# Threshold attention and an exact-GELU MLP on one core: diagonals moved to GpSimd, regrouping in longer runs, sums moved ahead

## The chip, the cores and the metric

The kernel runs on one core of a Trainium2 chip. The metric is the device time in microseconds (us) of one launch. Before the change it is 1428.99 us, the median of three runs (1428.49 to 1430.3). The profile was taken in another run, whose span is 1430.0 us.

Engines in the profile: PE is TensorE (matmuls), PEld its weight loads, DVE is VectorE, ACT is ScalarE, POOL is GpSimd, SP is SyncE, which here only issues DMAs. L12 is line 12 of the kernel.

## The reference

Attention with a threshold over 8 batches of 8 heads, 576 tokens, 64 channels; then an MLP with exact GELU on 4608 tokens, 512 to 2048 to 512 channels:

```python
scores = scale * np.matmul(q, k.transpose(0, 1, 3, 2))
thresh = np.max(scores, axis=-1, keepdims=True) - tau
scores = np.where(scores >= thresh, scores, -1000000000.0)
scores = scores - np.max(scores, axis=-1, keepdims=True)
attn = np.exp(scores)
attn = attn / (np.sum(attn, axis=-1, keepdims=True) + 1e-09)
o = np.matmul(attn, v)
x = o.transpose(0, 2, 1, 3).reshape(B * S, H * D)
h = x @ w_in
out = (0.5 * h * (1.0 + erf(h / sqrt(2)))) @ w_out
```

q, k, v are fp32. w_in and w_out lie in memory as 64-bit floats, so the kernel itself makes fp32 of them.

## The kernel before

**Order of work.** Heads are handled in pairs (A and B, the two halves of the 128 partitions): 32 pairs, four per batch. A pair has five slots: four chunks of 128 query rows and a tail of 64. In each slot TensorE makes the scores, VectorE the negated maximum, ScalarE Exp, VectorE the comparison with the threshold, the product and the sum of each row. Slots 0 to 19 are the first batch (pairs 0 to 3, called "early"); in them the weights are converted too, 32 pieces of 512 columns, part of them in each slot:

```python
def conversions():          # one piece; the yields are nanoseconds of VectorE
    vec.tensor_scalar(expo, hi, 0x7FF00000, None, op0=ALU.bitwise_and)           # L176
    nc.scalar.activation(power, expo, AF.Relu, bias=rebias, scale=8.0)           # L177
    yield 340
    vec.tensor_scalar(mant, top, 0x0FFFFFFF, 0x10000000, ...)                    # L183, the piece before
    yield 340
    vec.scalar_tensor_tensor(power, hi, 0x80000000, power, ...)                  # L185
    yield 720
    vec.scalar_tensor_tensor(dst, mant, 2.0 ** -28, power, ...)                  # L187
    load_piece()            # the next piece: two DMAs of 512 KB that GpSimd issues
    yield 700
```

Half of the pieces land in the first 2048 columns of the tiles `pd`, which from slot 20 on hold the turned p.

**Early pairs** divide p by its sum while they turn it: a matmul against a diagonal of the inverses. The slot's end, and what the next slot does with it:

```python
def softmax_tail(p, i):     # p = (scores >= threshold) * Exp, with the row sums in den
    nc.vector.scalar_tensor_tensor(row, sc, thr, row, is_ge, mult, accum_out=den[e])   # L386
    nc.gpsimd.tensor_scalar(den, den, 1e-9, None, op0=ALU.add)                         # L389

def diagonal(p, i):
    nc.vector.reciprocal(den, den)                                                     # L397
    for e in range(n):
        nc.scalar.activation(diag[:, e, :], ident, AF.Copy, scale=den[:, e:e + 1])     # L400

def turn_p_early(p, i):     # TensorE, in the next slot, behind its scores (L355)
    nc.tensor.matmul(tr, lhsT=w[:, cols], rhs=diag[:, e, :])                           # L301
    nc.scalar.copy(pT, tr)                                                             # L309
...
convert(3000 if n < 2 * HP else 3650 if n < BATCH - 1 else 1e9)     # end of each slot
if early:
    diagonal(p, i)
```

**Later pairs** turn p on VectorE in blocks of 32x32, and SyncE's DMAs bring the blocks to the partitions where the weighing of v needs them:

```python
def turn_p(p, i):           # pd[e] is [128, 20 blocks, 128]
    for e in reversed(range(n)):
        to = pd_tail[p % 2] if i == NC else pd[e][:, :, i * Q:(i + 1) * Q]
        nc.vector.transpose(to[:, 0:NB, :], w[:, e * S:(e + 1) * S] as [p, b, i])      # L433

def regroup(p, i):          # at i = 2 for chunks 0 and 1, at i = 3 for chunks 2 and 3, at 4 the tail
    half = slice((i - 1) * Q, (i + 1) * Q)
    for a in range(4):
        for e in (1, 0):
            nc.sync.dma_start(pT[e][:, :, a * P:(a + 1) * P][:, :, half], pd[e][rows, :, half])   # L448

def weigh_v(p, lo, hi):     # columns 0 to 288, 288 to 576
    nc.tensor.matmul(xT[f, 0:hi - lo], lhsT=v[:, e, c, :], rhs=pT[e][:, c, lo:hi])     # L460
    # then x = xT * inverse sums, on VectorE (L478)
```

**MLP.** Ten blocks of 256 tokens run as plain matmuls, cut into small steps that fill TensorE between the attention's (layer 1, L520; Gelu, L500, with the table of Exp loaded again behind it, L507; layer 2, L532). The last eight blocks, two by two, run with seven quarter products instead of eight (L641). For that, sums and differences of quarters are made on VectorE: of w_in in `weights_in()`, right behind the last slot, and four more of w_in and four of x at the start of the stage:

```python
fill(1e12, B * S)           # the rest of the plain blocks
strassen(*ext):
    vec.tensor_tensor(a, w_in_sb[c][:, low], a, op=ALU.subtract)     # 4 of them, L612
    x_sums(*DUOS[0])                                                 # 4 of them, L653 to L656
    for each duo of blocks: ...                                      # products, L641
    # out in rows of 512 channels, one DMA of 256 KB per 128 tokens (L744, L749)
```

Of the kernel before, what the change touches and what calls it, by code (L numbers as in the profile page):

```python
# [18 lines left out]
def kernel(  # L19
# [69 lines left out]

    ident = const.tile([P, P], FP32, name="ident")  # L90
# [5 lines left out]
    pd = [const.tile([P, 4 * KR, P], FP32, name=f"pd{e}") for e in range(2)]  # L96
# [6 lines left out]
    for t in pd:  # L103
        nc.gpsimd.memset(t[:, NB:4 * KR, :], 0.0)
# [32 lines left out]
    def load_piece():  # L137
        if loaded[0] == len(pieces):
            return
        dst, src = pieces[loaded[0]]  # L140
        loaded[0] += 1
        if not wide:
            nc.sync.dma_start(dst, src)
            converted[0] += 1
            load_piece()
            return
        k = loaded[0] - 1
        if k % 2:

            room = pd[k // 2 % 2][:, 0:NB - 2, :].bitcast(U32).rearrange("p b i -> p (b i)")  # L150
            raw, shifted = room[:, 0:2 * PIECE], room[:, 2 * PIECE:4 * PIECE]
        else:
            raw, shifted = (xg.tile([P, 2 * PIECE], U32, tag="x", name=s) for s in ("raw", "shifted"))
        nc.gpsimd.dma_start(raw, src.bitcast(U32))
        n = 8 * PIECE - 4
        nc.gpsimd.dma_start(shifted.bitcast(U8)[:, 0:n], src.bitcast(U8)[:, 3:3 + n])
        raws.append((dst, raw, shifted))
# [78 lines left out]
    def load_early(p):  # L236
        b, hp = divmod(p, HP)
        s = st[p] = {}
        for name, src in (("q", q), ("k", k)):
            t = s[name] = ld.tile([P, NC + 1, P], FP32, tag=name, name=name)  # L240
            eng = nc.scalar if p < 2 and name == "k" else nc.sync
            for e in range(2):
                eng.dma_start(
                    t[:, 0:NC, e * D:(e + 1) * D],
                    src[b, 2 * hp + e, 0:MAIN, :].rearrange("(t p) d -> p t d", p=P),
                )
            eng.dma_start(
                t[0:TAIL, NC, :].rearrange("p (e d) -> p e d", e=2),
                src[b, 2 * hp:2 * hp + 2, MAIN:S, :].rearrange("e s d -> s e d"),
            )  # L250

    def load_v_early(p):
        b, hp = divmod(p, HP)
        t = st[p]["v"] = v_sb[p % 4]
        for e in range(2):
            nc.sync.dma_start(t[:, e, 0:NC, :], v[b, 2 * hp + e, 0:MAIN, :].rearrange("(t p) d -> p t d", p=P))
            nc.sync.dma_start(t[e * TAIL:(e + 1) * TAIL, e, NC, :], v[b, 2 * hp + e, MAIN:S, :])
# [134 lines left out]
    def diagonal(p, i):  # L392

        s = st[p]
        den = s.pop(("sum", i))
        n = den.shape[1]
        nc.vector.reciprocal(den, den)  # L397
        diag = s["diag", i] = dg.tile([P, 2, P], FP32, tag="inv", name="diag")
        for e in range(n):
            nc.scalar.activation(diag[:, e, :], ident, AF.Copy, bias=0.0, scale=den[:, e:e + 1])  # L400
# [22 lines left out]
    def turn_p(p, i):  # L423

        s = st[p]
        w = s.pop(("p", i))
        n = 1 if i == NC else 2  # L430
        for e in reversed(range(n)):
            to = pd_tail[p % 2] if i == NC else pd[e][:, :, i * Q:(i + 1) * Q]
            nc.vector.transpose(to[:, 0:NB, :], w[:, e * S:(e + 1) * S].rearrange("p (b i) -> p b i", i=Q))  # L433

    def regroup(p, i):

# [3 lines left out]
        for a in range(4):  # L440
            rows = slice(a * Q, (a + 1) * Q)
            if i == NC:
                e, at = divmod(a * Q, TAIL)
                nc.sync.dma_start(s["pT"][e][:, :, MAIN + at:MAIN + at + Q], pd_tail[p % 2][rows])
                continue
            half = slice((i - 1) * Q, (i + 1) * Q)
            for e in (1, 0):
                nc.sync.dma_start(s["pT"][e][:, :, a * P:(a + 1) * P][:, :, half], pd[e][rows, :, half])  # L448

    def weigh_v(p, lo, hi):  # L450
# [5 lines left out]
        for c in range(KR):  # L456
            for e in range(2):
                f = slice(e * D, (e + 1) * D)
                pT = s["pT"][0 if p < EARLY and c == NC else e]
                nc.tensor.matmul(  # L460
                    xT[f, 0:hi - lo], lhsT=s["v"][:, e, c, :], rhs=pT[:, c, lo:hi],
                    start=(c == 0), stop=(c == KR - 1))
# [29 lines left out]
    warm = const.tile([P, 2], FP32, name="warm")  # L492
    nc.vector.memset(warm, 0.0)

# [15 lines left out]
    def block_steps(n):  # L510

        g = {}
        for j in range(N_DF):
# [11 lines left out]
        for m in range(TOK // P):  # L525
            for j in range(N_DF):
                yield NS_OUT, len(pieces) - N_DF + j + 1
# [11 lines left out]
    mlp = {"n": 0, "steps": None, "next": None, "debt": 0.0}  # L539
# [41 lines left out]
    def weights_in():  # L581
# [3 lines left out]
        rest = [units(v_sb[i % 4])[0] for i in range(NP - 4, NP - 1)]  # L585
# [9 lines left out]
        return (s1, s2, s4), room + rest  # L595
# [11 lines left out]
    def strassen(ext, room):  # L607
        s1, s2, s4 = ext
        for h in range(HF // U):
            for c in range(NK):  # L610
                a = w_in_sb[c][:, HF + h * U:HF + (h + 1) * U]
                vec.tensor_tensor(a, w_in_sb[c][:, h * U:(h + 1) * U], a, op=ALU.subtract)  # L612
        room = room + units(v_sb[(NP - 1) % 4]) + [u for t in pd_tail for u in units(t)]
        room += [x for _ in range(2) for x in unit(xg, "x", 2)]
        x_ext = [room.pop().rearrange("p (c t) -> p c t", c=NK) for _ in range(3)]
        o_ext = [room.pop() for _ in range(2)]
        room += [x for _ in range(N_DF // 2 + 2) for x in unit(gp, "g")]
        room += [u for t in pd for u in units(t)]
# [30 lines left out]
        def x_sums(n1, n2):  # L649
            t1, t2, t4 = x_ext  # L650
            a, b = x_blk[n1], x_blk[n2]
            b11, b21, b12, b22 = a[:, 0:NK, :], a[:, NK:2 * NK, :], b[:, 0:NK, :], b[:, NK:2 * NK, :]
            vec.tensor_tensor(t1, b12, b11, op=ALU.subtract)  # L653
            vec.tensor_tensor(t2, b22, t1, op=ALU.subtract)
            vec.tensor_tensor(b12, b22, b12, op=ALU.subtract)  # L655
            vec.tensor_tensor(t4, b21, t2, op=ALU.subtract)  # L656

# [7 lines left out]

        def finish_chunk(j, x, p3):
# [6 lines left out]
        x_sums(*DUOS[0])  # L673
        for sb, (n1, n2) in enumerate(DUOS):
# [45 lines left out]
            for m in ms:  # L720
# [3 lines left out]
                vec.tensor_tensor(lo[m][:, 0:HD], lo[m][:, 0:HD], vs[m], op=ALU.add)  # L724
            for n in DUOS[sb + 1] if sb + 1 < len(DUOS) else ():
                if n in away:
                    bring(n)
            if sb + 1 < len(DUOS):
                x_sums(*DUOS[sb + 1])
# [7 lines left out]
            for m in ms:  # L737
                product(ys[m], rows(g22, m, wt4))
                vec.tensor_tensor(hi[m][:, 0:HD], hi[m][:, 0:HD], ys[m], op=ALU.add)
            for m in ms:  # L740
                product(xs[m], rows(gs1, m, wt1))
                vec.tensor_tensor(hi[m][:, HD:2 * HD], hi[m][:, HD:2 * HD], xs[m], op=ALU.add)
                row = n2 * TOK + m * P
                nc.sync.dma_start(out[row:row + P, :], hi[m])  # L744
            for m in ms:
                product(xs[m], rows(g12, m, w_out_part(1, 1)))
                nc.scalar.copy(lo[m][:, HD:2 * HD], xs[m])
                row = n1 * TOK + m * P
                nc.sync.dma_start(out[row:row + P, :], lo[m])  # L749

    load_early(0)
    load_early(1)
# [12 lines left out]
    BATCH = HP * SLOTS  # L765
    WEIGH = 2
# [18 lines left out]
    for n in range(len(slots) + WEIGH + 1):  # L785
# [15 lines left out]
        if p > EARLY and i == WEIGH:  # L801
            made = [weigh_v(p - 1, h * HALF, (h + 1) * HALF) for h in range(2)]
# [34 lines left out]
        if n == BATCH:  # L837
            for t in pd_tail:
# [7 lines left out]
        convert(3000 if n < 2 * HP else 3650 if n < BATCH - 1 else 1e9)  # L846
        if early:
            diagonal(p, i)
        if not early:
# [51 lines left out]
```

## Time and profile before

Busy shares and instruction counts are in the first part of the page; the 40 slices show them along the time, in tenths. The costliest groups that the change touches, from the page and the groups of lines:

| line | engine, what | count | mean ns |
|---|---|---|---|
| L400 | ScalarE, diagonal 128x128 | 36 | 392 |
| L389 | GpSimd, sum + 1e-9, 1 or 2 columns | 20 | 233 to 891 |
| L397 | VectorE, reciprocal of 1 or 2 columns | 20 | 150 to 170 |
| L176, L183 | VectorE, 128x512, one input | 64 | 417 to 443 |
| L185, L187 | VectorE, 128x512, two inputs | 64 | 683 to 692 |
| L433 | VectorE, 128x576 turned in blocks | 252 | 756 to 779 |
| L460 | TensorE, weighing v, 288 columns | 1120 | 128 |
| L448 | SyncE, regroup DMA of 160 KB | 448 | 3.9 us to landing |

(A fp32 matmul is two instructions. The 128 ns of L460 are its busy time, 143.2 us, by its count; those of the two heads overlap.) The chain that ended last is 85% TensorE, 6% VectorE, 5% ScalarE and 2% DMA. Read the waits as: which engine stood still, in front of which line, until which engine's line ended. A stretch is read as its length, then the busy time of each engine in it.

### The profile page before, as it was taken

Reading aid. Unit: us, or ns where it says so; the run is one execution under the profiler, and the core shown is the slowest. Engines: PE = TensorE matmul, PEld = TensorE weight load, DVE = VectorE, ACT = ScalarE, POOL = GpSimd, SP = SyncE. Lnnn points to the kernel's source line nnn. Section 1 sums busy time; section 2 is a strip of 40 time slices with the busy share of each in tenths; the row PEclk is TensorE's granted clock in tenths of the full one; section 3 lists DMA queues with packets and bytes.
Section 4 is the critical chain, followed back from the end, with each engine's and each line's share of the span. In section 5 each row is a group of like instructions: output and inputs, shape, how many; then the busy total and the mean of one; then the engine's idle time right before and its main releaser. Section 6 shows DMA issues by size and latency. Waiting matters only on the chain.

```text
span 1430.0 us, 19776 instructions
## 1 busy us (share of the span) xinstructions
PE 1385.1 (97%) x6544; PEld 960.9 (67%) x6544; DVE 900.0 (63%) x1908; ACT 640.8 (45%) x1039; POOL 389.1 (27%) x810
## 2 busy tenths in 40 slices
PE   5898999999999999999999999999999999999999
PEld 4666547566466574665746657466488888888887
DVE  5887787777767777777777777777654142241230
ACT  5758525436256373562745627457142141230320
POOL 4443244433434434434434344330000000000000
PEclk8999999999999999999999999999999999999999
DMA  9977167776667776677776777765500100100000
GB/s 260 297 264 241 40 144 150 152 150 133 131 137 145 153 147 133 142 140 159 156 140 143 160 154 152 142 135 100 107 0 1 44 1 0 59 1 8 22 1 30
DMA packets 449492, 167.06 MB, mean 117 GB/s; under 512 B 413040, under 2 KB 432048, under 8 KB 449392
## 3 DMA queue, kind: packets, MB, share of 16 engines
q1 hardware_dynamic: 423184, 108.65, 38.8%
q0 software_dynamic: 23808, 56.57, 12.9%
q8 instruction: 53, 0.87, 0.2%
q10 hardware_dynamic: 2400, 0.59, 0.2%
q14 instruction: 47, 0.39, 0.1%
HBM read 71.68 MB, written 11.47 MB: 58 GB/s over the span
## 4 chain that ended last, share of the span: by engine, by line
PE 85%; DVE 6%; ACT 5%; DMA 2%; issue 1%; SPq 1%; POOL 0%; DVEq 0%; ACTq 0%; POOLq 0%
PE bank L641 27%; PE hT L520 18%; PE o_ps L532 17%; PE sc L355 12%; PE xT L460 9%; ACT p L370 2%; DVE p L386 1%; PE tr L301 1%; DVE nmx L367 1%; DVE power L185 1%; ACT L500 1%; ACT diag L400 1%; DMA pd<-in_moe_w_in_dram 1%; ACT L507 0%; DVE expo L176 0%
## 5 line engine op out<-in xcount | busy, mean ns | idle before, releaser
L370 ACT ACTIVATE p<-sc,nmx 128x576 f32<-128x576 f32 x288 | 202.5, 739 | 384.4 <-DVE nmx L367 384.4
L367 DVE TENSOR_REDUCE nmx<-sc 128x1 f32<-128x576 f32 x288 | 205.0, 749 | 149.8 <-PE sc L355 149.8
L520 PE MATMUL hT<-x,w_in 128*128 128x256 f32 x1280 | 296.2, 384 | 0.0
L532 PE MATMUL o_ps<-w_out,g 128*128 128x512 f32 x640 | 295.1, 604 | 0.0
L520 PEld LDWEIGHTS hT<-x,w_in 128*128 128x128 f32 x1280 | 238.4, 190 | 56.9 <-issue 25.2
L386 DVE SCALAR_TENSOR_TENSOR p<-sc,thr,p 128x576 f32<-128x576 f32 x288 | 225.4, 816 | 65.2 <-ACT p L370 64.2
L368 POOL TENSOR_SCALAR thr<-nmx,tau_eff 128x1 f32<-128x1 f32 x288 | 85.0, 295 | 547.4 <-DVE nmx L367 544.9
L532 PEld LDWEIGHTS o_ps<-w_out,g 128*128 128x128 f32 x640 | 117.1, 190 | 141.0 <-issue 139.2
L355 PE MATMUL sc<-kT,qT 64*128 64x288 f32 x960 | 165.0, 432 | 2.6 <-DVE p L386 2.4
L460 PE MATMUL xT<-pT,v 128*64 128x288 f32 (+2 forms) x1280 | 164.4, 409 | 3.2 <-ACT g L500 3.2
L433 DVE STREAM_TRANSPOSE pd<-p 128x576 f32<-128x576 f32 x224 | 160.8, 756 | 2.9
L355 PEld LDWEIGHTS sc<-kT,qT 64*128 64x128 f32 x960 | 92.9, 187 | 84.2 <-issue 71.8
L460 PEld LDWEIGHTS xT<-pT,v 128*64 128x64 f32 x1280 | 90.2, 137 | 73.4 <-issue 13.5
L232 POOL DMA_DIRECT2D v<-in_v_dram x208 | 111.0, 537 | 10.5 <-issue 9.5
L641 PE MATMUL bank<-x,w_in 128*128 128x256 f32 x384 | 94.7, 383 | 3.2 <-DVE x L655 3.2
L507 ACT ACT_TABLE_LOAD x71 | 91.1, 1283 | 1.3
L500 ACT ACT_TABLE_LOAD x71 | 91.1, 1283 | 1.3
L641 PE MATMUL bank<-unit 128*128 128x256 f32 x352 | 88.6, 382 | 0.0
L641 PEld LDWEIGHTS bank<-x,w_in 128*128 128x128 f32 x384 | 73.7, 192 | 14.2 <-issue 4.1
L223 POOL DMA_DIRECT2D q<-in_q_dram x104 | 70.9, 686 | 15.9 <-issue 15.0
L641 PEld LDWEIGHTS bank<-unit 128*128 128x128 f32 x352 | 67.4, 192 | 9.4
L301 PE MATMUL tr<-diag,p 128*128 128x128 f32 (+1 forms) x360 | 51.8, 312 | 22.1 <-ACT diag L400 13.8
(143 smaller groups left out, 1346.4 us busy)
## 6 DMA issues: line engine op xcount, KB each, us to landing
pT<-pd SPq DMA_DIRECT2D x448, 160.0 KB, 3.9
pT<-pd_tail SPq DMA_DIRECT2D x112, 80.0 KB, 2.8
q<-in_q_dram POOLq DMA_DIRECT2D x104, 72.0 KB, 4.0
k<-in_k_dram POOLq DMA_DIRECT2D x104, 72.0 KB, 2.6
out_dram<-o_sb SPq DMA_DIRECT2D x28, 256.0 KB, 3.9
inv<-turned SPq DMA_DIRECT2D x56, 128.0 KB, 3.9
v<-in_v_dram POOLq DMA_DIRECT2D x156, 40.0 KB, 3.0
raw<-in_moe_w_in_dram POOLq DMA_DIRECT2D x8, 512.0 KB, 5.5
```

The lines of the kernel that those rows point to most:

```text
L232: eng.dma_start(t[r:P:4, e, 0:n, :], rows[:, r * KR:r * KR + n, :])
L355: nc.tensor.matmul(sc[e][:, h, 0:HALF], lhsT=lhsT, rhs=s["kT"][rows, at:at + HALF], start=True, stop=True)
L367: nc.vector.tensor_reduce(nmx[:, e:e + 1], sc, axis=AXIS.XY, op=ALU.max, negate=True)
L370: nc.scalar.activation(w[:, e * S:(e + 1) * S].rearrange("p (h s) -> p h s", h=2), sc, AF.Exp, bias=nmx[:, e:e + 1], scale=1.0)
L386: nc.vector.scalar_tensor_tensor(row, sc[e][:, :, 0:HALF], thr[:, e:e + 1], row, op0=ALU.is_ge, op1=ALU.mult, accum_out=den[e])
L433: nc.vector.transpose(to[:, 0:NB, :], w[:, e * S:(e + 1) * S].rearrange("p (b i) -> p b i", i=Q))
L460: nc.tensor.matmul(xT[f, 0:hi - lo], lhsT=s["v"][:, e, c, :], rhs=pT[:, c, lo:hi], start=(c == 0), stop=(c == KR - 1))
L500: nc.scalar.activation(t, hT, AF.Gelu)
L507: nc.scalar.activation(warm[:, 1:2], warm[:, 0:1], AF.Exp)
L520: nc.tensor.matmul(hT[:, j % 2, :], lhsT=w_in_sb[c][:, j * P:(j + 1) * P], rhs=x_blk[n][:, c, :], start=(c == 0), stop=(c == N_DM - 1))
L532: nc.tensor.matmul(o[:, 0:d_model], lhsT=g[j][:, m * P:(m + 1) * P], rhs=w_out_sb[j], start=(j == 0), stop=(j == N_DF - 1))
L641: nc.tensor.matmul(to, lhsT=l, rhs=r, start=start and k == 0, stop=k == len(pairs) - 1, skip_group_check=not start)
```

## The change

1. **Diagonals.** In the first batch GpSimd multiplies the identity by the inverse sums, no longer ScalarE, and the reciprocal and the diagonals come after the first 700 ns of the slot's conversion instead of after all of it. This is to have them earlier and to free ScalarE.
2. **Regrouping.** The turned p of both heads is one tile, laid out so that a head's half (two chunks) is 20 x 64 floats in a row; pT is laid out in groups of 64 query rows, [9 groups, 5, 64]. A regroup DMA then moves runs of 5 x 64 floats, 1280 bytes, instead of 256. Both heads are turned in one instruction. The weighing takes 320 and 256 columns, and its right operand is now pieces of 64 columns, 320 apart.
3. **Sums.** The last w_in differences and the first sums of x are made behind the last slot too, while the last plain block is in its layer 2, which no longer reads w_in.
4. **Smaller parts.** k and v of the early pairs are loaded by four rows per partition, so v comes in runs of 1 KB; the table of Exp is loaded at the start; the outputs of the last stage are stored by halves of 256 channels, each as soon as it is there; unused blocks of the turned tile are set to zero at slot 20, not at the start.

```diff
-    pd = [const.tile([P, 4 * KR, P], FP32, name=f"pd{e}") for e in range(2)]
+    turned_p = const.tile([P, 2, 2, 4 * KR, 2 * Q], FP32, name="turned_p")
+    pd = [turned_p[:, e, :, :, :].rearrange("p h b i -> p (h b i)") for e in range(2)]
...
+                order = "(t p) d -> p t d" if name == "q" else "(p t) d -> p t d"
...
-            nc.scalar.activation(diag[:, e, :], ident, AF.Copy, bias=0.0, scale=den[:, e:e + 1])
+            nc.gpsimd.tensor_scalar(diag[:, e, :], ident, den[:, e:e + 1], None, op0=ALU.mult)
...
-        for e in reversed(range(n)):
-            to = pd_tail[p % 2] if i == NC else pd[e][:, :, i * Q:(i + 1) * Q]
-            nc.vector.transpose(to[:, 0:NB, :], w[:, e * S:(e + 1) * S].rearrange("p (b i) -> p b i", i=Q))
+        if i == NC:
+            nc.vector.transpose(pd_tail[p % 2][:, 0:NB, :], w[:, 0:S].rearrange("p (b i) -> p b i", i=Q))
+            return
+        nc.vector.transpose(
+            turned_p[:, :, i // 2, 0:NB, i % 2 * Q:(i % 2 + 1) * Q], w.rearrange("p (e b i) -> p e b i", e=2, i=Q))
...
-                nc.sync.dma_start(s["pT"][e][:, :, a * P:(a + 1) * P][:, :, half], pd[e][rows, :, half])
+                nc.sync.dma_start(by_64(s["pT"][e])[:, 2 * a + h, :, :], turned_p[rows, e, h, :, :])
...
-                    xT[f, 0:hi - lo], lhsT=s["v"][:, e, c, :], rhs=pT[:, c, lo:hi],
+                    rhs = by_64(s["pT"][e])[:, lo // (2 * Q):hi // (2 * Q), c, :]
...
+        # (in weights_in, behind the last slot)
+        assert mlp["n"] == PLAIN and mlp["layer"] == 2
         for h in range(HF // U):
             for c in range(NK):
                 a = w_in_sb[c][:, HF + h * U:HF + (h + 1) * U]
                 vec.tensor_tensor(a, w_in_sb[c][:, h * U:(h + 1) * U], a, op=ALU.subtract)
+        x_sums(x_ext, *DUOS[0])
...
-                row = n2 * TOK + m * P
-                nc.sync.dma_start(out[row:row + P, :], hi[m])
+                store(n2, m, hi[m], HD)
...
     load_early(0)
+    nc.scalar.activation(warm[:, 1:2], warm[:, 0:1], AF.Exp)
...
-            made = [weigh_v(p - 1, h * HALF, (h + 1) * HALF) for h in range(2)]
+            made = [weigh_v(p - 1, lo, hi) for lo, hi in ((0, WIDE), (WIDE, S))]
...
-        convert(3000 if n < 2 * HP else 3650 if n < BATCH - 1 else 1e9)
+        share = 3000 if n < 2 * HP else 3650 if n < BATCH - 1 else 1e9
         if early:
+            convert(700)
             diagonal(p, i)
+            share -= 700
+        convert(share)
```

## The prediction

> **What bounds the kernel now.** I read four views in this order: engine totals and the 40 slices of the page, then busy time by stretch, then the waits and the chain of waits of the stretches where TensorE is not full, and last the timeline at the one gap late in the run.
>
> ```profile
> PE 1385.1 (97%) x6544; PEld 960.9 (67%) x6544; DVE 900.0 (63%) x1908; ACT 640.8 (45%) x1039; POOL 389.1 (27%) x810
> ...
> PE   5898999999999999999999999999999999999999
> ...
> DVE  5887787777767777777777777777654142241230
> ...
> DMA  9977167776667776677776777765500100100000
> ```
>
> TensorE (PE) has work for 1385.1 of 1430.0 us. So 44.9 us is all that can be won without taking work from it, and the change takes none. The stretches say where those 44.9 us are (columns: stretch, its length, busy us of each engine with instruction counts, granted clock, DMA share, GB/s):
>
> ```profile
> 20.00:40.00 20.00, 16.50 (x114) 12.71 (x114) 16.55 (x37) 14.86 (x32) 8.81 (x19) 0.84 1.03 306
> 40.00:60.00 20.00, 15.58 (x105) 12.37 (x106) 17.34 (x39) 14.52 (x31) 7.92 (x16) 0.84 1.07 287
> 97.00:165.63 68.63, 60.37 (x331) 44.88 (x329) 49.57 (x111) 53.06 (x90) 20.18 (x42) 0.93 0.57 182
> 600.00:700.00 100.00, 99.75 (x480) 60.90 (x480) 75.03 (x155) 53.11 (x71) 40.35 (x82) 1.00 0.70 144
> 1020.00:1040.00 20.00, 16.77 (x68) 9.88 (x67) 9.55 (x18) 2.96 (x5) 0.00 (x0) 0.84 0.24 58
> ```
>
> From about 200 us to 1020 us TensorE is full (99.75 of 100 us in the row shown), whatever DMA (share 0.70) and VectorE (75) do. The losses lie in the first 200 us (about 35 us of idle TensorE, 11.8 of them in the first 20 us, before data is there), at 1020 to 1040 us (3.2 us, clock 0.84), and after the last product (3.4 us).
>
> The first 20 slots, the first batch, run from 11.43 to 165.63 us. Their waits, first for 21 to 97 us, then for 97 to 166 us (engine and line that waited, what for, us in total, times, longest):
>
> ```profile
> PEld tr L301 <- ACT diag L400: 16.8, 8, 6.2
> PE tr L301 <- ACT diag L400: 13.2, 6, 5.6
> DVE p L386 <- ACT p L370: 4.9, 10, 1.1
> DVE expo L176 <- DMA raw<-in_moe_w_in_dram: 2.1, 1, 2.1
> ```
> ```profile
> PE tr L301 <- ACT g L500: 5.0, 4, 2.3
> DVE mant L183 <- ACT power L177: 6.2, 3, 3.6
> DVE nmx L367 <- PE sc L355: 4.9, 2, 3.7
> DVE p L386 <- ACT p L370: 3.9, 8, 0.9
> ```
>
> And three steps of the chain of waits (start, us, what):
>
> ```profile
> 34.50 0.46 DVE expo L176
> 35.06 0.55 issue
> 35.61 0.68 ACT diag L400 x2
> 36.32 0.75 ACT p L370
> ```
>
> The reader is to see that TensorE waits for the diagonals, the diagonals stand in ScalarE's queue, and behind them in the same queue stands the Exp of the next slot, for which VectorE then waits. Until 97 us VectorE is nearly the bound (67.3 of 75.4 us busy, summed over slots). After that ScalarE joins it: Gelu with two table loads (1.28 us each) comes into every slot.
>
> Last, the join of the plain blocks and the seven-product stage, in the timeline:
>
> ```profile
> 1030.31 1.03 PE L641 MATMUL bank<-x,w_in 128*128 128x256 f32 x4
> 1034.34 0.69 DVE L656 TENSOR_TENSOR unit<-x,unit 128x512 f32<-128x512 f32 x1
> 1034.57 2.04 PE L641 MATMUL bank<-x,w_in 128*128 128x256 f32 x4 [3.23 <-DVE x L655]
> 1036.40 1.91 PE L641 MATMUL bank<-unit 128*128 128x256 f32 x4
> ```
>
> TensorE stops for 3.23 us because four w_in differences and four x sums come only then, and goes on at half speed.
>
> **What the Trainium skill says.** (1) "TensorE: Matmul & The Clock Gate", section "What's actually happening": an idle window of about 3.4 us halves TensorE's clock until a busy window has passed. The trace agrees: after the 3.23 us stop the groups of four instructions start 1.83 and 1.71 us apart, and 0.86 us apart some 5 us later. (2) "GPSIMD Engine Reference", section "1. Specifications": GpSimd shares its SBUF interfaces with VectorE and contends with instructions that use two ports or two SBUF inputs. The trace agrees: the addition on two columns (den, L389) takes 0.23 to 0.89 us, and at 31.63 us it ends (32.25) just as VectorE's mantissa operation does (32.22). (3) The same page, section "4.1 Engine selection": one-input work runs on GpSimd at roughly line rate. Only the 128x128 select that builds the identity, 0.29 us, bears on this. (4) "DMA: Bandwidth & Descriptors", section "Specifications": 512 B or more are wanted for line rate. The page counts 413,040 of 449,492 packets under 512 B, but no run here shows yet what longer ones bring.
>
> **The change part by part.**
>
> Diagonals on GpSimd, inside the conversion. Removed from ScalarE: 36 instructions of 0.39 us, 0.69 us per full slot. Added to GpSimd: 36 of an estimated 0.3 to 0.5 us (from the 0.29 us select), plus up to some 0.5 us of waiting for VectorE's port. The reciprocal moves from behind about 3.2 to 3.9 us of conversion to behind 0.7 us of it. Before, a diagonal is ready about 3.5 (conversion) + 0.2 + 0.7 = 4.4 us after the slot's sums; after, about 0.9 (the addition, which 0.7 us of conversion nearly hides) + 0.2 + 1.5 = 2.6 us, and 1.2 us later where the issue of two weight loads stands before it on GpSimd. So it is there before VectorE begins the next slot, and the wait for it on TensorE goes. Only what shortens the slot counts:
> - Slots 1 to 11 (21.57 to 97 us): VectorE is idle for 8.1 us. About 0.22 us per slot (its own maximum to the Exp behind it) must stay, 2.4 us, and the weight DMAs' 3.1 us go only in part. I take 4 us back.
> - Slots 12 to 19 (97 to 165.63 us): VectorE is idle 19.1 us and ScalarE 15.6 us, so no engine is full and the loop between them is the bound. ScalarE loses eight slots' diagonals, some 4.7 us; the trace's chain holds 3.2 us of them directly. With the earlier turns of p I take 7 us.
> - Against it: VectorE's reciprocal can now wait for GpSimd's addition, and the two share ports: 20 slots by 0.1 us, 2 us.
> Sum: 9 us. TensorE's total work is fixed, so every microsecond by which the first batch ends sooner moves all that follows.
>
> Exp's table loaded at the start, v and k by four rows per partition. The table load at 6.42 us (1.28 us) is overlapped by TensorE's own transposes, which end at 8.4 us. It is worth 0.1 us. Eight loads of v go from 256 B runs to 1 KB, k still writes 256 B pieces. DMA is at share 1.0 until 60 us, so some of the 3.1 us waits for weights may shrink: 0.5 us.
>
> Regrouping by 1280 B, A and B (the two heads of a pair) turned at once. A regroup DMA of 160 KB has 640 runs of 256 B, then 128 of 1280 B. 448 of them: 286,720 packets become 57,344, so the total should fall to about 220,000. The issue on SyncE (eight in 7.43 us, 0.93 us each) gets shorter. 224 transposes (0.72 us each in a row) become 112 of an estimated 1.3 to 1.4 us, some 10 us less of VectorE. All this lies in stretches where TensorE is full: 0 us. Weighing v in 320 and 256 columns instead of 288 and 288 is the same 576 columns: 0 us.
>
> Sums behind the last slot. VectorE ends its twelve w_in sums at 1023.83 us and then waits until 1029.13 for the divisors. Eight more operations of 0.62 to 0.69 us, 5.2 us, fit in that hole almost to the microsecond. The 3.23 us stop goes, and with it the slow stretch: five groups from 1034.57 to 1041.75 us take 7.18 us where 5 x 0.86 = 4.3 us would do, 2.9 us. Sum: 6.1 us.
>
> Stores by halves. The last store moves 128 KB, not 256 KB; its tail (last copy ends 1427.04, span 1430.0) shortens by perhaps 0.3 us.
>
> Total: 9 + 0.6 + 0 + 6.1 + 0.3 = 16 us, and 1428.99 - 16 = 1413.
>
> **Rivals.** First, VectorE as the bound of the first batch: if GpSimd's 128x128 operations and VectorE's conversions hold each other up, as the 0.23 to 0.89 us of the addition warns, the slots keep their length, or grow by 0.3 us each, and only the join is won: 1421 to 1425. Second, the strided right operand: weighing now reads five or four pieces of 64 columns, 1280 B apart. If TensorE reads these slower, by a tenth of the 164 us of L460, the full stretch grows by some 14 us and eats all: 1427. Nothing in the trace before has such an operand; against it speaks that no other operand shape shows any cost of its own. Third, false waits: one tile for both heads, with the weight conversion's room inside it, could make the transposes or the weight loads wait for the regroup DMAs. In the trace before, heads' transposes wait 2.9 us in all, so there is no such wait now. It would show as VectorE time, of which the full stretch has 25% to spare: 0 to 5 us. Fourth, the larger gain: if the earlier diagonals break the loop in the second half altogether, its slots go from 8.6 us to VectorE's 6.5 us, and 10 us more come: 1403.
>
> **Range and chances.** The join is nearly sure (6 us), the first batch is the open part (0 to 19 us), the strided operand is a small chance of a loss. Range 1404 to 1423. For 2% it would have to be below 1400.4, for which all of the first batch's removable idle time would have to go: 0.06. Above 1457.6 only with a wait that nothing in the trace suggests: 0.02.
>
> **What would show it.** Right: no wait of the turned p (L301) for a diagonal; slot 20 starting some 9 to 10 us sooner than 165.63; no stop of TensorE at the join, and its clock at 1.0 there; packets near 220,000, DMA share near 0.4 in the full stretch, and 100 us stretches in the middle unchanged in matmuls per 100 us. Wrong: xT's matmuls longer than 128 ns per instruction of 288 columns in proportion; diagonals on GpSimd above 1 us; VectorE's operations longer than 0.42 and 0.69 us in the conversion; the reciprocal waiting for GpSimd.

## The result and the profile after

| | us, median | range | slot 20 starts at, us |
|---|---|---|---|
| before | 1429.19 | 1428.49 to 1430.3 | 165.63 |
| changed | 1426.2 | 1425.97 to 1426.96 | 168.47 |

Each row is the median of four runs; the fourth run of the kernel before moves its median from 1428.99 to 1429.19. The ratio is 0.9979 (95% interval 0.9962 to 0.9997): about 3.0 us less, where 16 were predicted. The last column is from the profiles: the first batch ends 2.8 us later, not 9 to 10 sooner. The profiled run of the kernel before took 1432.14 us, almost 3 us above its median, and that of the changed kernel 1425.97 us, so the two profiles differ by more (5.8 us) than the medians.

The page of the changed kernel, engine totals and DMA:

```profile
span 1424.2 us, 19643 instructions
...
PE 1384.0 (97%) x6544; PEld 960.4 (67%) x6544; DVE 894.5 (63%) x1788; ACT 629.0 (44%) x1004; POOL 417.7 (29%) x848
...
DMA packets 219347, 167.05 MB, mean 117 GB/s; under 512 B 122480, under 2 KB 203952, under 8 KB 219248
```

TensorE has the same 6544 instructions, GpSimd (POOL) has 28.6 us more, ScalarE 11.8 less. The packets are halved, as predicted. Busy time by stretch, columns as before:

```profile
20.00:40.00 20.00, 14.96 (x105) 10.94 (x104) 14.76 (x32) 11.04 (x22) 11.34 (x20) 1.00 0.92 289
40.00:60.00 20.00, 17.75 (x114) 13.12 (x114) 18.05 (x40) 13.28 (x28) 13.58 (x23) 0.83 0.93 270
600.00:700.00 100.00, 99.75 (x480) 60.78 (x479) 74.90 (x142) 53.69 (x71) 41.85 (x85) 1.00 0.65 144
1020.00:1040.00 20.00, 20.00 (x96) 13.12 (x96) 13.95 (x28) 5.50 (x12) 0.00 (x0) 1.00 0.27 63
```

The last row shows the gain: TensorE is full at the join, at clock 1.0. In the row of 600 to 700 us TensorE is as before to the hundredth. In the first row both TensorE and VectorE do less than before (16.50 and 16.55), and in the second they do more (before: 15.58 and 17.34). Fixed stretches don't show the loss of the first batch; stretches cut at its slots, further down, do.

The waits of the first batch, again for 21 to 97 us and then for 97 to 166 us:

```profile
PE sc L356 <- DVE p L387: 7.3, 6, 2.8
DVE p L387 <- POOL thr L369: 5.2, 7, 1.6
PEld tr L302 <- POOL diag L401: 4.6, 6, 1.7
...
PE tr L302 <- POOL diag L401: 2.0, 2, 1.1
```
```profile
POOL diag L401 <- PE tr L302: 9.9, 4, 3.8
...
DVE mant L185 <- ACT power L179: 5.7, 3, 3.3
PE tr L302 <- ACT g L509: 5.5, 4, 2.5
```

TensorE's waits for a diagonal have indeed shrunk, in the first stretch from 16.8 us (weight loads) and 13.2 us (matmuls) to 4.6 and 2.0. In their place TensorE now stands 7.3 us in front of the next scores, until VectorE's p is done, and the batch became longer. That alone doesn't show that the old waits were off the path, because GpSimd's cost came in at the same time; e2 below separates the two. The waits for Gelu and for the conversion's power in the second stretch are about as they were.

The join in the timeline of the changed kernel:

```profile
1027.49 3.70 PE L543 MATMUL o_ps<-w_out,g 128*128 128x512 f32 x8
1031.02 1.89 PE L663 MATMUL bank<-x,w_in 128*128 128x256 f32 x8
1032.75 1.03 PE L663 MATMUL bank<-v,unit 128*128 128x256 f32 x4
1033.61 1.03 PE L663 MATMUL bank<-v,w_in 128*128 128x256 f32 x4
```

No stop; groups of four start 0.86 us apart from the beginning. From the first of these products to the end of the span it is now 1424.2 - 1031.02 = 393.2 us; before it was 1430.0 - 1030.31 = 399.7. This stage gave 6.5 us. If 3.0 are measured in all, about 3.5 are lost ahead of it. The two profiles alone don't show so much, since the profiled run before was a long one. The run e8 below has the code of the kernel before up to the last slot, and its profiled run lies at its median: it starts slot 20 at 164.27 us and the join at 1028.28. Against that the changed kernel is 4.2 us later at slot 20 and 2.7 us later at the join.

Where the time goes is to be seen at the end of slot 1 on GpSimd (start, us, what, idle before and releaser; the last three columns of an issue are its tile, source and count):

```profile
24.63 0.61 POOL L390 TENSOR_SCALAR den<-den 128x2 f32<-128x2 f32 x1 [1.47 <-DVE p L387]
25.62 2.25 POOL L401 TENSOR_SCALAR diag<-ident,den 128x128 f32<-128x128 f32 x2 [0.38 <-PE sc L356]
27.82 0.59 POOL L156 DMA_DIRECT2D raw<-in_moe_w_in_dram  x1
...
28.95 0.53 POOL L156 DMA_DIRECT2D turned_p<-in_moe_w_in_dram  x1
```

The first of these issues in the kernel before:

```profile
25.78 0.61 POOL L154 DMA_DIRECT2D raw<-in_moe_w_in_dram  x1
```

And on VectorE of the changed kernel, at the end of slot 1 and in slot 2:

```profile
26.28 0.51 DVE L185 TENSOR_SCALAR mant<-shifted 128x512 uint32<-128x512 uint32 x1
...
27.43 0.74 DVE L189 SCALAR_TENSOR_TENSOR w_in<-mant,power 128x512 f32<-128x512 uint32 x1
...
33.09 0.43 DVE L178 TENSOR_SCALAR expo<-raw 128x512 uint32<-128x512 uint32 x1 [1.11 <-DMA raw<-in_moe_w_in_dram]
...
37.71 0.43 DVE L178 TENSOR_SCALAR expo<-turned_p 128x512 uint32<-128x512 uint32 x1 [2.47 <-DMA turned_p<-in_moe_w_in_dram]
38.05 1.42 DVE L368 TENSOR_REDUCE nmx<-sc 128x1 f32<-128x576 f32 x2
```

Two diagonals take 2.25 us and stand ahead of the issue of the next weight loads, which begins at 27.82 us instead of 25.78 before. VectorE then stands 1.11 and 2.47 us for weights in slot 2. That slot (from maximum to maximum) lasts 9.96 us, where it was 6.57 before.

### The profile page after: what moved, and what is told of

It reads as the page before. It is cut to its first block, busy times and chain, and to the rows that moved or that the text cites. A ratio compares the mean times of both kernels' runs of the same rounds, so it can differ in the third digit from the quotient of the medians.

```text
span 1424.2 us, 19643 instructions
## 1 busy us (share of the span) xinstructions
PE 1384.0 (97%) x6544; PEld 960.4 (67%) x6544; DVE 894.5 (63%) x1788; ACT 629.0 (44%) x1004; POOL 417.7 (29%) x848
## 4 chain that ended last, share of the span: by engine, by line
PE 86%; DVE 5%; ACT 4%; DMA 2%; POOL 2%; issue 1%; SPq 0%; DVEq 0%; POOLq 0%; ACTq 0%
PE bank L663 27%; PE o_ps L543 18%; PE hT L530 18%; PE sc L356 12%; PE xT L473 10%; ACT p L371 1%; DVE p L387 1%; DVE nmx L368 1%; PE tr L302 1%; ACT L509 1%; POOL diag L401 1%; DMA q<-in_q_dram 1%; DVE power L187 1%; DMA turned_p<-in_moe_w_in_dram 1%; ACT L516 0%
## 5 line engine op out<-in xcount | busy, mean ns | idle before, releaser
L356 PE MATMUL sc<-kT,qT 64*128 64x288 f32 x960 | 168.2, 435 | 5.2 <-DVE p L387 4.7
L473 PE MATMUL xT<-pT,v 128*64 128x256 f32 (+1 forms) x1280 | 165.4, 412 | 2.7 <-ACT g L509 2.7
L434 DVE STREAM_TRANSPOSE turned_p<-p 128x1152 f32<-128x1152 f32 x112 | 154.1, 1376 | 3.0
L663 PE MATMUL bank<-w_out,unit 128*128 128x256 f32 x416 | 92.4, 380 | 0.0
L663 PEld LDWEIGHTS bank<-w_out,unit 128*128 128x128 f32 x416 | 79.3, 191 | 10.5
L225 POOL DMA_DIRECT2D k<-in_k_dram x104 | 69.7, 675 | 0.7 <-DMA inv<-turned 0.3
```

The source lines that it names most:

```text
L225: eng.dma_start(t[e * D + f:e * D + f + Q], rows[:, :, f:f + Q])
L356: nc.tensor.matmul(sc[e][:, h, 0:HALF], lhsT=lhsT, rhs=s["kT"][rows, at:at + HALF], start=True, stop=True)
L434: nc.vector.transpose(turned_p[:, :, i // 2, 0:NB, i % 2 * Q:(i % 2 + 1) * Q], w.rearrange("p (e b i) -> p e b i", e=2, i=Q))
L473: nc.tensor.matmul(to, lhsT=s["v"][:, e, c, :], rhs=rhs, start=(c == 0), stop=(c == KR - 1))
L663: nc.tensor.matmul(to, lhsT=l, rhs=r, start=start and k == 0, stop=k == len(pairs) - 1, skip_group_check=not start)
```

## The experiments

The theory after the result: TensorE's waits for diagonals were off the path, and GpSimd, doing them inside the conversion, costs more than it frees. The rivals: the single room that two successive diagonals share ties VectorE or GpSimd to TensorE; the place inside the conversion costs on any engine; GpSimd's thresholds, standing behind the diagonals, hold VectorE; the new order of loads costs. Edits are to the changed kernel unless said otherwise. Ratios are to the kernel before, with 95% intervals; slot 20 is its start in the profile.

| run | us | ratio | slot 20 |
|---|---|---|---|
| e1_scalar_behind | 1421.49 | 0.9949 (0.9931 to 0.9967) | 162.64 |
| e2_scalar_within | 1421.48 | 0.9941 (0.9922 to 0.9960) | 165.32 |
| e3_vector_within | 1433.82 | 1.0029 (1.0018 to 1.0040) | 177.00 |
| e4_only_diagonals | 1432.11 | 1.0018 (1.0011 to 1.0025) | 166.35 |
| e5_gpsimd_two_rooms | 1426.68 | 0.9982 (0.9976 to 0.9989) | 169.21 |
| e6_scalar_two_rooms | 1422.76 | 0.9948 (0.9933 to 0.9963) | 166.03 |
| e7_gpsimd_twice | 1439.43 | 1.0074 (1.0062 to 1.0086) | 182.72 |
| e8_only_sums | 1423.78 | 0.9961 (0.9948 to 0.9973) | 164.27 |
| e9_threshold_on_scalar | 1428.34 | 0.9999 (0.9991 to 1.0007) | 172.25 |
| e10_no_gelu_early | 1412.78 | 0.9887 (0.9874 to 0.9901) | 156.11 |
| e11_old_load_order | 1421.70 | 0.9947 (0.9934 to 0.9959) | 164.72 |
| e12_gpsimd_behind | 1423.62 | 0.9963 (0.9950 to 0.9977) | 162.96 |

Slot 20 comes from one profiled run, which can lie beside the median (e1: 1420.99 us, e11: 1423.09 us, with equal medians), so it is read only together with the median.

### The diagonals undone: e1, e2

e1 takes the first part of the change back, engine and place; e2 only the engine.

```diff
-            nc.gpsimd.tensor_scalar(diag[:, e, :], ident, den[:, e:e + 1], None, op0=ALU.mult)
+            nc.scalar.activation(diag[:, e, :], ident, AF.Copy, bias=0.0, scale=den[:, e:e + 1])
 # e1 only:
+        convert(share)
         if early:
-            convert(700)
             diagonal(p, i)
-            share -= 700
-        convert(share)
```

> The changed kernel with its diagonals as before: on ScalarE, behind the slot's conversion. GpSimd theory (the diagonals take 0.93 us on GpSimd instead of 0.39 on ScalarE and hold up the weight loads and thresholds queued behind them, so that slot 20 starts at 168.5 us instead of 165.6): slot 20 starts at 165 to 166 us, time 1422.5 to 1424. Rival (the new order of k and v, the early table load or the common tile of the turned p lengthen the first batch): slot 20 stays at 168 us and the time at 1426.

> The changed kernel with the diagonals on ScalarE but early, within the conversion. If an early diagonal is worth what the prediction said (some 4 us in slots 1 to 11) and only GpSimd spoiled it: slot 20 starts at 160 to 163 us, time 1419 to 1421. If the wait of TensorE for the diagonals was never what set the slots' length: slot 20 at 165 to 166.5 us, the same as with the diagonals behind the conversion, time 1422.5 to 1424.

Both take 1421.5 us: 4.7 us less than the changed kernel, 7.7 less than before. That is faster than either theory expected of e1, and for e2 between the two. The runs of each span 5 us, so a gain of 1 or 2 us from the early place could hide in them, the predicted one could not. The first part of the change is a loss of 4.7 us, and without it this version beats both kernels. The waits of e1 and then of e2 (21 to 170 us) say why the diagonals' waits misled:

```profile
PEld tr L302 <- ACT diag L401: 19.0, 12, 3.6
...
PE tr L302 <- ACT diag L401: 13.2, 8, 2.8
DVE p L387 <- ACT p L371: 8.8, 19, 0.9
```
```profile
DVE p L387 <- ACT p L371: 7.3, 20, 0.9
...
PEld tr L302 <- ACT diag L401: 3.2, 6, 0.7
```

In e1 TensorE's weight loads wait 19.0 us for diagonals (its matmuls 13.2 us, for the most part the same stops). In e2 nearly all of that is gone, 3.2 us are left, and the time is the same. The stretches by slots show what else fills them (VectorE alone: length, its busy time and instructions, clock, DMA share, GB/s; slots 1 and 2, slots 3 to 11, slots 12 to 19). First the kernel before, then the changed kernel, then e1:

```profile
21.57:34.93 13.36, 11.59 (x27) 0.82 1.00 300
34.93:95.45 60.52, 54.32 (x124) 0.94 0.91 280
95.45:165.63 70.18, 50.97 (x115) 0.93 0.58 185
```

```profile
21.34:38.05 16.71, 11.80 (x27) 1.00 0.89 279
38.05:99.89 61.84, 55.70 (x122) 0.92 0.81 265
99.89:168.47 68.58, 51.24 (x113) 0.98 0.60 188
```
```profile
21.50:35.03 13.53, 11.56 (x28) 1.00 1.02 293
35.03:94.05 59.02, 54.14 (x124) 0.97 0.91 286
94.05:162.64 68.59, 50.96 (x114) 1.00 0.58 190
```

Against e1 the changed kernel loses 3.2 us in slots 1 and 2 (weights that come late), 2.8 in slots 3 to 11, of which 1.6 is VectorE busy longer, and nothing in slots 12 to 19. These shares are from single runs: e11, with e1's median, has 14.19, 60.53 and 68.61 us, so each may be off by 1 to 2 us. In e1's slots 3 to 11 VectorE is idle 4.9 of 59 us, and what it waits for there is mostly the slot's Exp (4.5 us). Little was left for an earlier diagonal to win: e2 shortens VectorE's wait for Exp by 1.5 us (lists above), but its wait for the next scores grows by 1.4 (4.8 to 6.2 us), and slots 3 to 11 take 59.83 us. Its slots 12 to 19 take 71.14 us, as in e6, while the times of e1 and e2 agree; where those 2.5 us come back was not traced.

### On VectorE itself: e3

```diff
-            nc.gpsimd.tensor_scalar(diag[:, e, :], ident, den[:, e:e + 1], None, op0=ALU.mult)
+            nc.vector.tensor_scalar(diag[:, e, :], ident, den[:, e:e + 1], None, op0=ALU.mult)
```

> The changed kernel with the diagonals on VectorE, within the conversion, an estimated 0.2 us each. GpSimd theory: the queue of GpSimd is free again and ScalarE too; against it 36 x 0.2 = 7 us more of VectorE in the first batch, whose slots 1 to 11 it nearly fills: slot 20 at 164 to 168 us, time 1421 to 1425. If ScalarE's diagonals set the length of slots 12 to 19, these get shorter by 0.7 us each against the ones of the kernel before; if the loop of Gelu, table loads and banks sets it, they stay at 8.6 us.

1433.8 us, 4.6 more than before. One diagonal takes 0.286 us on VectorE (median), and 36 of them keep it busy for 9.0 us. The wait list of VectorE (21 to 166 us) has more:

```profile
DVE diag L401 <- PE tr L302: 14.0, 5, 4.7
```

All diagonals lie in one room, so the next may be written only when TensorE has read the last; inside the conversion that is early, and on the busiest engine it stops everything behind it. It raised the question whether the same room costs GpSimd, whose diagonals wait 9.9 us for the same matmuls (second list above).

### The first part alone: e4

To the kernel before, only the GpSimd line and the new place:

```diff
-            nc.scalar.activation(diag[:, e, :], ident, AF.Copy, bias=0.0, scale=den[:, e:e + 1])
+            nc.gpsimd.tensor_scalar(diag[:, e, :], ident, den[:, e:e + 1], None, op0=ALU.mult)
+        share = 3000 if n < 2 * HP else 3650 if n < BATCH - 1 else 1e9
         if early:
+            convert(700)
             diagonal(p, i)
+            share -= 700
+        convert(share)
```

> The kernel before with only the diagonals changed (GpSimd, within the conversion). GpSimd theory: slot 20 at 168 to 169 us instead of 165.6, time 1431 to 1433, slower than before. Rival (other parts lengthen the first batch): slot 20 at 163 to 166 us, time 1427 to 1429.

2.6 us slower than before (1.6 to 3.6). The loss is there without any other part, somewhat smaller than the 4.7 us seen from the other side. With the 5.6 us that the sums alone win (e8, below) it makes the 3.0 us that were measured.

### Two rooms: e5, e6

```diff
-        diag = s["diag", i] = dg.tile([P, 2, P], FP32, tag="inv", name="diag")
+        k = two["k"] = 1 - two["k"]           # two["room"]: one tile of [P, S] under the same tag
+        diag = s["diag", i] = two["room"][:, k * 2 * P:(k + 1) * 2 * P].rearrange("p (e x) -> p e x", e=2)
 # e6 also has e2's line on ScalarE
```

> The changed kernel with two rooms for the diagonals in turn, where there was one. In the changed kernel GpSimd stands for 10.9 us in front of a new diagonal until TensorE has read the old one. If that single room is what spoils the early diagonal: those waits are gone, slot 20 starts at 162 to 165 us instead of 168.5, time 1421 to 1423.5. If the length of the work on GpSimd (0.93 us each) and the queue behind it do: the waits go, but slot 20 stays at 167 to 169 us and the time at 1425 to 1427.

> The diagonals on ScalarE, within the conversion, in two rooms. If the single room took away what an early diagonal is worth (ScalarE within the conversion was no faster than behind it, 1421.5 us both): slot 20 at 159 to 162 us, time 1416 to 1419. If TensorE's wait for diagonals never set the slots' length: 1420.5 to 1422.5.

1426.7 and 1422.8 us, against 1426.2 and 1421.5 with one room. So the wait for the room isn't GpSimd's cost, and e6 shows that a diagonal made as early as can be, with no room to wait for, on an engine that makes it in 0.39 us, brings nothing over one that comes behind the conversion. By now four kernels with diagonals on ScalarE (e1, e2, e6 and e11, below) lie at 1421.5 to 1422.8 us, and two with early diagonals on GpSimd at 1426.2 and 1426.7.

### Each diagonal twice: e7

```diff
+            for _ in range(2):
-            nc.gpsimd.tensor_scalar(diag[:, e, :], ident, den[:, e:e + 1], None, op0=ALU.mult)
+                nc.gpsimd.tensor_scalar(diag[:, e, :], ident, den[:, e:e + 1], None, op0=ALU.mult)
```

> The changed kernel with every diagonal made twice on GpSimd (the second into the same place; the result is the same): 36 more operations of 0.9 us, 33 us more of GpSimd in the first batch. GpSimd's length and queue: the step from ScalarE to GpSimd cost 4.7 us, so as much again or more, 5 to 12 us: slot 20 at 173 to 180 us, time 1431 to 1438. If only the single room counted: slot 20 at 168 to 171 us, time 1426 to 1428.5.

1439.4 us, 13.2 more than the changed kernel. GpSimd's diagonals take 59.1 us instead of 33.2, so about half of the 25.9 us added in this place goes into the time. VectorE's list (21 to 166 us) names the place:

```profile
DVE p L387 <- POOL thr L369: 26.6, 14, 3.1
```

The slot's threshold, which GpSimd also makes, comes behind the diagonals (8.7 us of such waits in the changed kernel).

### The threshold taken from GpSimd: e9

```diff
+            if p >= EARLY:
                 nc.gpsimd.tensor_scalar(thr, nmx, -1.0, tau_eff, op0=ALU.mult, op1=ALU.subtract)
...
             # behind the Exp of the slot
+            if p < EARLY:
+                nc.scalar.activation(thr, nmx, AF.Identity, bias=minus_tau, scale=-1.0)
```

> The changed kernel, diagonals on GpSimd, but in the first batch the threshold of each row (one column, L369) made by ScalarE behind its Exp instead of by GpSimd, so that it no longer queues behind diagonals and weight loads. In the changed kernel VectorE waits 8.7 us for that threshold between 21 and 166 us (0.5 us with the diagonals on ScalarE). If this is how GpSimd's diagonals cost time: the wait goes, slot 20 starts at 162 to 165 us, time 1421 to 1423.5. If it is the weight loads issued late (VectorE waits 3.6 us for them): slot 20 stays at 166.5 us or later and the time at 1424.5 to 1427.

1428.3 us: slower than the changed kernel by 2, which neither theory expected. The wait on GpSimd is gone and another of the same size has come (VectorE, 21 to 166 us):

```profile
DVE p L392 <- ACT thr L377: 8.3, 18, 1.0
...
DVE expo L180 <- DMA raw<-in_moe_w_in_dram: 3.7, 1, 3.7
```

In the changed kernel VectorE waits 8.7 us for the threshold and 2.7 for Exp, together 11.4; in e1 it waits 0.5 and 8.8, together 9.3. So most of the threshold's wait only stands where the wait for Exp would stand anyway. And slots 12 to 19 went from 68.58 to 71.99 us, 3.4 us, with 13 operations of 0.28 us on ScalarE, 3.6 us in sum. That they lie in the loop of the second half and show in full is the likely reading, not a shown one. The late weights of slot 2 are still there.

### GpSimd, but behind the conversion: e12

```diff
+        convert(share)
         if early:
-            convert(700)
             diagonal(p, i)                    # GpSimd's line is kept
-            share -= 700
-        convert(share)
```

> The changed kernel with its diagonals on GpSimd, but behind the slot's conversion, where the kernel before had them. The slot's weight loads are then issued before them, and VectorE is not converting beside them (0.61 us each, as in the changed kernel where VectorE stands still, instead of 1.0 to 1.2). If the place is what costs (loads issued 2 us late, slot 2 lasting 10.0 us instead of 6.6): slot 2 at 6.6 to 7 us, slot 20 at 163 to 165.5 us, time 1421.5 to 1423.5. If the engine costs wherever it stands (the next slot's thresholds then queue behind 1.2 us of diagonals, and TensorE gets them later): slot 20 at 167 us or later, time 1425 to 1429.

1423.6 us, with a wide range (1421.5 to 1426.6), 2.6 less than the changed kernel. Its profiled run is among the shortest (1421.64 us), and in it the slots are much as in e1 (12.77, 60.08 and 68.75 us). The diagonals by tile (count, then min/median/max ns, first and last start), in the changed kernel:

```profile
L401 POOL TENSOR_SCALAR diag<-ident,den x36: 607/868/1382, 16.5 to 167.0; 128x128 f32<-128x128 f32 x36
```

and in e12, with GpSimd from the end of slot 1 to slot 2 under it:

```profile
L401 POOL TENSOR_SCALAR diag<-ident,den x36: 598/614/635, 21.6 to 163.2; 128x128 f32<-128x128 f32 x36
...
25.43 0.61 POOL L156 DMA_DIRECT2D raw<-in_moe_w_in_dram  x1
...
26.78 0.54 POOL L156 DMA_DIRECT2D turned_p<-in_moe_w_in_dram  x1
...
28.26 1.21 POOL L401 TENSOR_SCALAR diag<-ident,den 128x128 f32<-128x128 f32 x2 [0.42 <-DVE den L398]
```

The same instruction takes 0.60 to 0.64 us, always, though VectorE runs the next slot's maximum (two of 0.70 us, which read the scores from PSUM) beside it. The weights are issued first, at 25.43 us, and slot 2 lasts 6.14 us. So the early place alone costs nothing that these runs show (e2), GpSimd alone perhaps 2 us or nothing (2.1 us above e1, with overlapping intervals and similar slots), and the two together 4.7 us.

### The loop of the second half: e10

```diff
 # e1, and in the first batch (slots below 20):
-            nc.scalar.activation(t, hT, AF.Gelu)
+            nc.scalar.activation(t, hT, AF.Copy if early_gelu else AF.Gelu)
-            dirty[0] = True                   # Exp's table is loaded again behind it
+            dirty[0] = dirty[0] or not early_gelu
```

This leaves out the Gelu of the MLP blocks made in the first batch: a copy of the same size stands in its place, and no table is loaded there.

> As e1 (diagonals on ScalarE behind the conversion), but Gelu left out in the first batch: a plain copy in its place, with no table loads, so the outputs of the first block are not those of the reference. If the loop of ScalarE (Exp, Gelu with two table loads, copies of the turned p, then TensorE's next scores) sets slots 12 to 19, these shrink from 8.6 to some 7 us, slot 20 starts at 148 to 154 us and the time falls to 1408 to 1415. If VectorE or the weights' conversion sets them: slot 20 at 160 to 163 us, time 1420 to 1422.

1412.8 us, 8.7 less than e1. Slots 12 to 19, all engines, in e10:

```profile
97.05:156.11 59.06, 56.65 (x338) 43.09 (x337) 50.71 (x114) 35.10 (x72) 20.59 (x44) 1.00 0.72 220
```

and in e1:

```profile
94.05:162.64 68.59, 57.62 (x338) 43.03 (x337) 50.96 (x114) 54.46 (x93) 20.65 (x44) 1.00 0.58 190
```

Without Gelu and its tables TensorE is nearly full there (56.65 of 59.06 us). So the predicted loop is real, and in these slots it is worth 9.5 us, but its links are Gelu and its two table loads, not the diagonals. (Slots 3 to 11 took 3.0 us more in this profile than in e1's, so slot 20 starts 6.5 us sooner.) In the changed kernel ScalarE has 4.1 us less to do in these slots than in e1 (50.38 against 54.46 us), and they take 68.58 and 68.59 us: so ScalarE makes the diagonals in a gap of its own. How much of the 9.5 us is Gelu and how much its tables, e10 doesn't tell apart.

### The other parts: e8, e11

e8 is the kernel before with the third part alone (the four last w_in differences and the first sums of x made behind the last slot). e11 is e1 with k and v loaded in the old order.

```diff
 # e8, to the kernel before: from strassen() to weights_in()
+                vec.tensor_tensor(a, w_in_sb[c][:, h * U:(h + 1) * U], a, op=ALU.subtract)
+        x_sums(x_ext, *DUOS[0])
 # e11, to e1:
-                order = "(t p) d -> p t d" if name == "q" else "(p t) d -> p t d"
+                order = "(t p) d -> p t d"
-            nc.sync.dma_start(t[:, e, 0:NC, :], v[...].rearrange("(p t) d -> p t d", p=P))
+            nc.sync.dma_start(t[:, e, 0:NC, :], v[...].rearrange("(t p) d -> p t d", p=P))
```

> The kernel before with only the sums made behind the last slot. If the trace reads right (6.3 us from the end of the first batch to the end of the run), 1422.5 to 1424 us, TensorE without a stop at the join. If the join gives something back later (VectorE's divisions for the last pair delayed by 5 us), less than 5 us: above 1424.

> As e1, with the early k and v in the old order of rows (256 B runs of v again). If the longer runs are worth something in the crowded first 60 us: 0.5 to 2 us slower than e1's 1421.5, with slots 1 to 4 later. If not: 1421 to 1422.

e8: 1423.8 us, 5.6 less than before (3.9 to 7.4). From the first product of the join to the end it is 1421.7 - 1028.28 = 393.4 us, against 399.7. The sums alone are the gain of this change. e11: 1421.7, equal to e1; the order of the loads is worth nothing. What remains of the change (regrouping, turning both heads at once, halves in the stores, Exp's table) lies between e8 and e1: 2.3 us, with intervals that overlap. 0.2 of it is in the last stage (393.2 for 393.4 us); the rest wasn't settled.

## Why the prediction was wrong

**Where it was wrong: the term "Sum: 9 us" of the diagonals.** The failed step is the one from "the wait for it on TensorE goes" to slots that are 11 us shorter. The wait did go, for the most part (e2: 3.2 us left of 19.0), and nothing was gained, because other waits stand in the same slots. So the term is 0 for early diagonals on ScalarE, and on GpSimd a loss of 3 to 5 us (e4 +2.6; changed against e1 +4.7). Of its three lines:

- "Slots 1 to 11 ... I take 4 us back": 0. The 8.1 us of idle VectorE were read as if the diagonals ahead of Exp in ScalarE's queue caused them. The chain of waits did hold such a step, but with the diagonals early VectorE's wait for Exp falls by 1.5 us only, its wait for the scores grows by as much, and the time stays (e2 and e6 no faster than e1). The 0.22 us per slot that "must stay" is 0.5 (4.5 us in nine slots of e1), and VectorE's list for slots 3 to 11 has only one other wait, 1.1 us for weights.
- "Slots 12 to 19 ... I take 7 us": 0 (68.58 in the changed kernel, 68.59 with the diagonals back on ScalarE in e1, 68.75 in e12). That the profile before has 70.18 us is not the moved diagonals' doing, since e1 is as short without them. A loop was rightly seen, but a link was credited that has slack in it. e10 shows which links have none.
- "2 us against it": about 6 in the profiles (3.2 in slots 1 and 2, 2.8 in slots 3 to 11). The operation was put at 0.3 to 0.5 us, from a select of 0.29, plus up to 0.5 of waiting; it takes 0.61 us undisturbed, where VectorE needs 0.286, so the "roughly line rate" that the prediction takes from the Trainium skill ("GPSIMD Engine Reference", section "4.1 Engine selection") doesn't hold for it, and 0.93 on average within the conversion. The text saw that the weight loads' issue and the diagonals share a queue ("1.2 us later where the issue of two weight loads stands before it"), but only in one direction: at the end of slot 1 the diagonals stand ahead of the issue. And the port was counted as a wait of VectorE's reciprocal, while VectorE's conversion was simply slower (1.6 us in slots 3 to 11).

The first rival named this ("if GpSimd's 128x128 operations and VectorE's conversions hold each other up", slots longer by 0.3 us, 1421 to 1425), and the kernel came 1 us above its range; two of the named signs came too, diagonals above 1 us and longer operations in the conversion. How much of the loss is the port and how much the late issue in later slots wasn't separated: no run had the diagonals early on GpSimd and the loads issued by another engine.

The bound was off as well: "44.9 us is all that can be won" takes TensorE's busy time as fixed, but part of it is the slow clock. The same 6544 instructions are busy for 1385.1 us in the profile before and 1376.7 in that of e1; in slots 12 to 19 it is 61.92 us at clock 0.93 and 57.62 at 1.00, for 338 instructions each.

**Where it held.** The join: predicted 6.1 and 0.3 for the stores, 6.5 us in the profile; for the sums alone 6.3 in e8's profile and 5.6 in its time. TensorE's stop had two costs, the 3.23 us and the slow clock behind it, and both went. (The stop is a little shorter than the window of about 3.4 us that the prediction cites, and the slow groups followed all the same.) The regrouping: 0 us in the full stretch, with 100 us in the middle unchanged, and packets at 219,347. The second rival, the strided operand, is dead, in the groups by shape of the changed kernel (busy us, mean ns):

```profile
L434 DVE STREAM_TRANSPOSE turned_p<-p 128x1152 f32<-128x1152 f32 x112 | 154.1, 1376 | 3.0
...
L473 PE MATMUL xT<-pT,v 128*64 128x320 f32 x640 | 93.2, 438 | 0.0
...
L473 PE MATMUL xT<-pT,v 128*64 128x256 f32 x640 | 76.6, 386 | 2.7 <-ACT g L509 2.7
```

and of the kernel before, whose early pairs use the same sizes with operands in one piece:

```profile
L460 PE MATMUL xT<-pT,v 128*64 128x320 f32 x80 | 11.7, 437 | 0.0
L460 PE MATMUL xT<-pT,v 128*64 128x256 f32 x80 | 9.5, 384 | 0.0
```

438 for 437 ns, 386 for 384. The wide transposes take 154.1 us where 10 us less than before was estimated (6.7 less, in stretches where TensorE is full). The third rival, false waits in the full stretch, doesn't show either: VectorE is busy 74.90 of 100 us there, before 75.03.

**Small terms.** Loads and Exp's table: predicted 0.6, the load order measured at nothing. DMA share in the full stretch: "near 0.4" was predicted from the packets, and it is 0.65 (before 0.70).

## What to carry to other kernels

A wait in the list, even one in the chain, is worth its length only if no other wait stands right behind it, for the engine that waits or for the one that it hands to. First ask which engine of the stretch has no idle time that could go, and take away the suspected link in a copy of the kernel. Before moving work to an engine with little to do, look at what stands behind it in that engine's queue (here the issue of loads, and a threshold that the busiest engine needs in every slot) and at what runs beside it at that moment (here VectorE's conversion). Parts that are sure, as the sums here, should be measured alone: with the diagonals left where they were, the rest of this change brings 7.7 us instead of 3.0.

## What the runs showed of the hardware

- GpSimd's multiplication of 128x128 by a column takes 0.61 us with VectorE idle (two in 1.21 us at 16.46 us of the changed kernel), 0.61 beside VectorE's maximum over scores in PSUM (e12), and up to 1.38 beside the conversion, whose operations have two inputs in SBUF or one (two in 2.25 us in the lines above). The Trainium skill, "GPSIMD Engine Reference", section "1. Specifications", names VectorE's instructions with two SBUF inputs, or in a mode with two ports, as those that contend with GpSimd; the durations agree with it, and no run tells the two apart. VectorE pays far less: at the end of slot 1 a two-input operation goes from 0.69 to 0.74 us, a one-input one from 0.42 to 0.51.
- Runs five times as long between two places in SBUF halve the packets and hardly change the rest: share 0.70 to 0.65, 144 GB/s in both, 3.9 to 3.6 us to landing. The same skill, "DMA: Bandwidth & Descriptors", section "Why small descriptors are slow (HBM only)", says that transfers from SBUF to SBUF don't suffer from small descriptors; the traces agree.
- A moving operand in pieces of 64 columns, 1280 bytes apart, costs TensorE nothing measurable.
